# Seven products in place of eight also for the second matrix product of the experts

## The chip, the cores and the metric

The kernel runs on one core of a Trainium2 chip. The metric is device time of one execution in microseconds; the median of three runs of the kernel before is 2268.2 us (2265.57 to 2270.24). The profile comes from one further execution, which took 2266.92 us.

## The reference

Three layers follow each other on 2304 tokens of 512 features: attention with a memory (4 batches, 8 heads, 576 positions), a gated feed-forward layer, and a dense mixture of 8 experts. The change is in the mixture:

```
logits = x @ w_gate;  P = exp(logits - max), then 8 times rows and columns normalised (Sinkhorn)
for e in range(8):
    h = maximum(x @ w1[e], 0)          # 2304x512 @ 512x1024
    out += P[:, e:e+1] * (h @ w2[e])   # 2304x1024 @ 1024x512
```

All is float32. Each matrix product is computed as three products of rounded parts: a number is split into a high part (rounded to the fast matmul's format) and a low part (the rest), and high x high, high x low and low x high are added.

## The kernel before, in words

The mixture (moe2) works through 16 units: a unit is half of an expert's 1024 hidden features, 512 of them. In a unit it goes through four pairs of 512 tokens and a last group of 256 tokens.

**Hidden products.** x W1 of a pair is a product of 2x2 blocks by the Strassen-Winograd scheme, with seven products in place of eight (unit_hidden). Operands are blocks (A11, A12, A21, A22) of W1 and sums of them (S1 to S4), and seven parts of x per pair. The seven parts of x are made once, written to DRAM by parts (L583), and read back for each unit into five right-side buffers (xr, L1027). One such product is 12 matmuls with 256 moving columns and a new 128x128 stationary tile each (L904). Results gather in PSUM: a bank named chain (pool pc), and banks of pool pt. ScalarE copies the chain aside (keep, L911), VectorE adds (L916), ScalarE takes relu into the high part of h (L923), and VectorE makes its low part (L924). For the last 256 tokens (last_hidden, L956) all eight block products are made, 48 matmuls.

**Output products.** h W2 is computed without the scheme (unit_out, L976): 128 tokens by 512 output features, 12 matmuls with 512 moving columns, in one bank of pool poc, called an output chunk below. VectorE adds the bank, scaled by the token's weight, to the accumulator of the outputs (L992, in unit 0 a copy, L988).

**Order.** moe2 writes the order of TensorE's queue out by hand: "HHOHHOHHOHO" for a pair, H a hidden product of this pair and O an output chunk of the pair before; "HOOHOO" for the last 256 tokens. After each letter a step of other work may be issued (behind): the next unit's weights (prepare_unit, L819) or, in unit 0, the logits, the fourth pair's parts of x, and the Sinkhorn steps. prepare_unit loads 2 MB of raw weights through SP's queue (L825), GpSimd makes S1 to S4 (L845), ScalarE the high parts (L834, L839), VectorE and GpSimd the low parts (L835, L841). Engines run their own queues in order; tc.issue_after fixes a place in the queue only, it isn't a wait.

## Time and profile before

| | us |
|---|---|
| median of three runs | 2268.2 |
| profiled execution | 2266.92 |
| its span in the profile | 2264.8 |
| first hidden product of the mixture starts at | 723.13 |
| second unit starts at | 836.87 |

The span is the part of the execution that the profile covers, and times inside it count from its start. Busy times of engines overlap; a matmul's duration in the timeline includes its way through the array, so consecutive matmuls overlap, and the spacing of their starts is what they cost. A row of the timeline merges equal neighbours ("x12"), its idle time before them and what ended it stand in brackets.

### The profile page before, as it was taken

The numbers are of one execution on the slowest core, as the hardware profiler recorded it, in microseconds if no ns is written. First come the engines' busy times: TensorE is split into PE (matmuls) and PEld (weight loads), VectorE is DVE, ScalarE is ACT, GpSimd is POOL, SyncE is SP. The second block draws the span as 40 slices with busy tenths as digits, with TensorE's granted clock in tenths as the row PEclk, the third lists the DMA queues.
The fourth block names the chain that finished last, engine by engine and source line by source line (L and its number), as shares of the span: only waits on it lengthen the run. The fifth ranks groups of instructions, "written<-read, shape, count | busy, mean of one in ns | idle before, by whom it ended". The sixth has DMA issues, their size and how long they took to land.

```text
span 2264.8 us, 33872 instructions
## 1 busy us (share of the span) xinstructions
PE 2219.6 (98%) x13490; PEld 1904.9 (84%) x13490; DVE 1205.4 (53%) x1915; ACT 735.0 (32%) x1452; POOL 466.7 (21%) x425
## 2 busy tenths in 40 slices
PE   7999999999999899999999999999999999999999
PEld 4555677888888789989899898998989989899898
DVE  8999898442413655444454444544445444454433
ACT  6777733322312312222222222222222222232221
POOL 6766665210201121101011010110101101011000
PEclk9999999999999999999999999999999999999999
DMA  5322276357533836546465464654646546465463
GB/s 188 119 93 78 100 253 214 132 203 259 199 118 117 282 112 233 197 148 224 148 230 197 150 223 146 229 195 156 223 144 230 196 157 218 146 229 199 159 203 132
DMA packets 112956, 406.46 MB, mean 179 GB/s; under 512 B 12448, under 2 KB 12448, under 8 KB 109728
## 3 DMA queue, kind: packets, MB, share of 16 engines
q1 hardware_dynamic: 112800, 404.30, 52.5%
q8 instruction: 108, 1.77, 0.3%
q14 instruction: 48, 0.39, 0.1%
HBM read 364.92 MB, written 39.32 MB: 178 GB/s over the span
## 4 chain that ended last, share of the span: by engine, by line
PE 80%; DVE 2%; DMA 2%; POOL 1%; issue 1%; ACT 0%; SPq 0%; POOLq 0%; ACTq 0%; DVEq 0%
PE po L474 39%; PE pt L904 15%; PE pc L904 11%; PE p L474 9%; PE pt L967 4%; DMA xp<-xl 1%; DMA raw<-w 1%; POOL na L503 1%; PE pp L474 1%; POOL ws L845 0%; DVE na L488 0%; DVE w L835 0%; DMA graw<-gvo 0%; DVE nb L491 0%; DVE nb L492 0%
## 5 line engine op out<-in xcount | busy, mean ns | idle before, releaser
L474 PE MATMUL po<-w,h 128*128 128x512 f32 x3456 | 834.4, 392 | 4.2 <-DVE xacc L988 4.2
L474 PEld LDWEIGHTS po<-w,h 128*128 128x128 f32 x3456 | 631.8, 188 | 126.2 <-DVE xacc L988 4.5
L904 PE MATMUL pt<-xr,w 128*128 128x256 f32 x3072 | 403.8, 280 | 5.0 <-DMA xr<-xp 4.9
L904 PEld LDWEIGHTS pt<-xr,w 128*128 128x128 f32 x3072 | 381.7, 188 | 13.6 <-DVE w L841 5.1
L992 DVE SCALAR_TENSOR_TENSOR xacc<-po,Pw,xacc 128x512 f32<-128x512 f32 x270 | 202.2, 749 | 272.2 <-PE po L474 272.1
L474 PE MATMUL p<-xs,gw 128*128 128x512 f32 (+1 forms) x1440 | 306.9, 370 | 6.5 <-DVE sg L639 3.6
L904 PEld LDWEIGHTS pc<-xr,w 128*128 128x128 f32 x2304 | 296.8, 188 | 15.0 <-ACT m L911 0.2
L904 PE MATMUL pc<-xr,w 128*128 128x256 f32 x2304 | 304.3, 280 | 0.0
L474 PEld LDWEIGHTS p<-xs,gw 128*128 128x128 f32 x1440 | 251.9, 189 | 55.3 <-DVE sg L639 4.9
L911 ACT COPY m<-pc 128x512 f32<-128x512 f32 x192 | 112.2, 584 | 510.0 <-PE pc L904 509.8
L916 DVE TENSOR_TENSOR m<-pt,m 128x512 f32<-128x512 f32 x256 | 175.0, 688 | 182.8 <-PE pt L904 121.3
L923 ACT ACTIVATE h<-m 128x512 fp32r<-128x512 f32 x256 | 161.4, 633 | 263.5 <-DVE m L916 256.3
L924 DVE SCALAR_TENSOR_TENSOR h<-m,h 128x512 fp32r<-128x512 f32 x256 | 191.8, 754 | 70.5 <-ACT h L923 65.8
L835 POOL TENSOR_TENSOR w<-raw,w 128x512 fp32r<-128x512 f32 x17 | 22.5, 1323 | 755.0 <-ACT w L834 755.0
L841 POOL TENSOR_TENSOR w<-raw,w 128x512 fp32r<-128x512 f32 x32 | 57.3, 1792 | 472.1 <-ACT w L839 472.1
L474 PE MATMUL po<-h,ws 128*128 128x512 f32 x576 | 137.4, 390 | 0.0
L474 PEld LDWEIGHTS po<-h,ws 128*128 128x128 f32 x576 | 108.0, 188 | 23.0
L835 DVE TENSOR_TENSOR w<-ws,w 128x512 fp32r<-128x512 f32 x64 | 66.4, 1039 | 79.3 <-ACT w L834 77.0
L322 POOL TENSOR_SCALAR P<-P,sums 128x576 f32<-128x576 f32 (+4 forms) x160 | 92.3, 591 | 26.4 <-ACT Z L392 12.1
L503 POOL TENSOR_SCALAR na<-na 128x512 f32<-128x512 f32 x36 | 87.1, 2434 | 47.6 <-ACT na L502 47.4
L967 PEld LDWEIGHTS pt<-xr,w 128*128 128x128 f32 x768 | 94.4, 188 | 2.7
L967 PE MATMUL pt<-xr,w 128*128 128x256 f32 x768 | 95.3, 279 | 0.0
(186 smaller groups left out, 1930.2 us busy)
## 6 DMA issues: line engine op xcount, KB each, us to landing
xr<-xp SPq DMA_DIRECT2D x480, 512.0 KB, 4.1
raw<-w SPq DMA_DIRECT2D x64, 512.0 KB, 6.1
gw<-kg SPq DMA_DIRECT2D x24, 1024.0 KB, 4.8
graw<-gvo SPq DMA_DIRECT2D x36, 512.0 KB, 4.3
xp<-xl SPq DMA_DIRECT2D x30, 512.0 KB, 3.3
kg<-gw SPq DMA_DIRECT2D x24, 512.0 KB, 3.9
ws<-ko SPq DMA_DIRECT2D x24, 512.0 KB, 3.8
qk<-qkv SPq DMA_DIRECT2D x16, 640.0 KB, 3.9
```

The costliest lines, as they stand in the source:

```text
L322: nc.gpsimd.tensor_scalar(t, t, r, 1.0, op0=ALU.mult, op1=ALU.mult)
L474: self.nc.tensor.matmul(out, lhs[a], rhs[b], start=start and n == 0, stop=stop and n == 2, skip_group_check=shared)
L503: nc.gpsimd.tensor_scalar(t, t, pattern(0x40000000), pattern(0x4FEFFE00), op0=ALU.max, op1=ALU.min)
L835: lo.tensor_sub(t[:, 1], q[name], f32(t[:, 0]))
L841: engine.tensor_sub(t[:, 1, j], raw[:, 2 * n + j, 1], f32(t[:, 0, j]))
L904: nc.tensor.matmul(out[:, j * HT:(j + 1) * HT], w[:, a, j, k], x[:, b, k], start=start and j + k + n == 0, stop=k + n == 3, skip_group_che ...
L911: nc.scalar.copy(t, src)
L916: nc.vector.tensor_add(c, *terms)
L923: nc.scalar.activation(t[:, 0], c, AF.Relu)
L924: nc.vector.scalar_tensor_tensor(t[:, 1], c, 0.0, f32(t[:, 0]), op0=ALU.max, op1=ALU.subtract)
L967: nc.tensor.matmul(ph[:, j * HT:(j + 1) * HT], w[:, b, j, k], x[:, c, k], start=j + a + k + i == 0, stop=a + k + i == 4, skip_group_check= ...
L992: nc.vector.scalar_tensor_tensor(acc, po, weight, acc, op0=ALU.mult, op1=ALU.add)
```

## The change

h W2 of units 1 to 15 is now a product of 2x2 blocks with seven products as well. The blocks of h (A11, A12, A22; A21 only within sums) and the sums s1 to s4 of them are the stationary side; blocks of W2 (B11, B21, B22) and sums T1 to T4 are the moving side, 256 columns wide. unit_out is a generator: each step issues one product for a pair (two times 128 tokens, 12 matmuls) or for the last 256 tokens (6 matmuls), and two or one accumulations of 128x256 from PSUM into the outputs. The banks pu and pq hold partial results that go on being added to after they have been read. Unit 0 keeps whole chunks (first_out).

The hidden products come in the order A11, A12, S2, S1, S4, S3, A22; S2, S1 and S4 add to the chain, A22 adds to the bank of S3. A letter H begins with tick, which issues low parts and sums put off from the letters before (later). The order is "HO" seven times, "HOOHOOHOOHO" for the last 256 tokens; unit 0 keeps its own for pairs. prepare_unit has gates: after S3, S2, T3 and B11 it waits for the last 256 tokens (1), and before T2, T4, T1, B21, B22 for the next unit's first pair (2). PSUM is split into four pools of two banks (pu, pq, pt, pc). In unit 0 the fourth pair's parts come before the logits. The core of the diff:

```diff
--- before.py
+++ after.py
@@ -602,13 +602,13 @@
         yield
         t3 = new()
         sub(t3, b22, b12)
-        self.part(pool, t4, to[5])
-        yield
-        self.part(pool, t3, to[4])
+        self.part(pool, t4, to[6])
+        yield
+        self.part(pool, t3, to[5])
         yield
         self.part(pool, b21, to[1])
         yield
-        self.part(pool, b22, to[6])
+        self.part(pool, b22, to[4])
         yield
     def moe1(self, last):
...
     def prepare_unit(self, u):
+        low = []
+        for gate in self.unit_steps(u, low):
+            yield gate
+            while low:
+                low.pop(0)()
+        for what in low:
+            what()
+    def unit_steps(self, u, low):
...
+        q = {}
+        for i in range(2):
+            for j in range(2):
+                q[f"A{i + 1}{j + 1}"] = raw[:, 2 * i:2 * i + 2, 0, j * HT:(j + 1) * HT]
+                q[f"B{i + 1}{j + 1}"] = raw[:, 2 * i:2 * i + 2, 1, j * HT:(j + 1) * HT]
+        def split(t, src, lo):
+            nc.scalar.copy(t[:, 0], src)
+            low.append(lambda: lo.tensor_sub(t[:, 1], src, f32(t[:, 0])))
+        def parts(name, lo=nc.vector):
+            w1[name] = self.w1p.tile([P, 2, 2, HT], F32R, name="w1")
+            split(w1[name], q[name], lo)
+        def parts2(name, lo=nc.vector):
+            t = self.w2p.tile([P, 2, 512], F32R, name="xl")
+            w2[name] = t.rearrange("p a (j n) -> p a j n", j=2)
+            split(w2[name], q[name], lo)
...
+        for _ in range(8 if u else 0):
             yield
+        total("S3", sub, "A11", "A21")
+        yield
+        parts("S3")
+        yield
+        total("S1", add, "A21", "A22")
+        yield
+        total("S2", sub, "S1", "A11")
+        yield
+        parts("S2")
+        yield
+        total("S4", sub, "A12", "S2")
+        yield
...
+        total("T3", sub, "B22", "B12")
+        parts2("B11", nc.gpsimd)
+        yield
+        parts2("T3")
+        yield
+        yield 1
+        for name in ("A11", "A12", "S1", "S4", "A22"):
+            parts(name)
             yield
+        total("T1", sub, "B12", "B11")
         parts("A21", nc.gpsimd)
         yield
+        total("T2", sub, "T1", "B22")
+        yield
+        yield 2
+        parts2("T2")
+        total("T4", add, "B21", "T2")
+        yield
+        parts2("T4")
+        yield
+        parts2("T1")
+        yield
+        parts2("B21", nc.gpsimd)
+        yield
+        parts2("B22")
+        yield
+    def later(self, steps, what):
+        self.todo.append((self.now + steps, what))
+    def tick(self):
+        self.now += 1
+        due = [t for t in self.todo if t[0] <= self.now]
+        self.todo = [t for t in self.todo if t[0] > self.now]
+        for _, what in due:
+            what()
+    def split_h(self, h, name, src, relu, n=512):
+        t = self.hp.tile([P, 2, 512], F32R, name="h")[:, :, 0:n]
+        if relu:
+            nc.scalar.activation(hi, src, AF.Relu)
+            self.later(1, lambda: nc.vector.scalar_tensor_tensor(lo, src, 0.0, f32(hi), op0=ALU.max, op1=ALU.subtract))
+        else:
+            nc.scalar.copy(hi, src)
+            self.later(1, lambda: nc.vector.tensor_sub(lo, src, f32(hi)))
...
         chain = self.pc.tile([P, 512], F32, name="pc")
         one = lambda: self.pt.tile([P, 512], F32, name="pt")
         mm(chain, "A11", xs(0), True)
         m1 = keep(chain)
-        yield h
+        yield
         m2 = one()
         mm(m2, "A12", xs(1), True)
-        result((0, 0), m2, m1)
-        yield h
+        c11 = plus(m2, m1)
+        self.split_h(h, "A11", c11, True)
+        yield
         mm(chain, "S2", xs(2))
         u2 = keep(chain)
-        split()
-        mm(chain, "S3", xs(4))
+        yield
+        mm(chain, "S1", xs(3))
         u3 = keep(chain)
...
+        mm(chain, "S4", xs(4))
+        if u:
+            r21 = new()
+            nc.scalar.activation(r21, chain, AF.Relu)
+        yield
+        m7 = one()
+        mm(m7, "S3", xs(5), True)
+        if u:
+            s3 = new()
+            relu(s3, c11, r21, ALU.subtract)
+            self.split_h(h, "S3", s3, False)
+        c22 = plus(m7, u3)
+        self.split_h(h, "A22", c22, True)
+        yield
+        mm(m7, "A22", xs(6))
+        if u:
+            s1 = r21
+            relu(s1, c22, r21, ALU.add)
+            self.split_h(h, "S1", s1, False)
+        c21 = plus(m7, u2)
+        self.split_h(h, "A12", c21, True)
+        def rest():
+            s2 = c11
+            relu(s2, c11, s1, ALU.subtract)
+            self.split_h(h, "S2", s2, False)
+            def last():
+                s4 = c21
+                relu(s4, c21, s2, ALU.add)
+                self.split_h(h, "S4", s4, False)
+            self.later(1, last)
+        if u:
+            self.later(1, rest)
+        yield
...
+                if j == 0:
+                    yield
+            t = self.mp.tile([P, 512], F32, name="m")
+            nc.scalar.activation(t, ph, AF.Relu)
+            r.append(t.rearrange("p (j t n) -> p j t n", j=2, t=2))
+            if i == 0:
+                (a11, a21) = (r[0][:, :, k] for k in range(2))
+                self.split_h(h, "A11", a11, False, n)
+                s3 = self.half_tile()
+                nc.vector.tensor_sub(s3, a11, a21)
+                self.split_h(h, "S3", s3, False, n)
+            else:
+                (a12, a22) = (r[1][:, :, k] for k in range(2))
+                s1 = self.half_tile()
...
+    def first_out(self, p, h, t, c):
...
+    def unit_out(self, u, p, h):
...
+        for a, b, bank, i, d in (
+            ("A11", "B11", "pu", 0, 0), ("S3", "T3", "pq", 1, 1), ("S2", "T2", "pu", 1, 0), ("A22", "T4", "pq", 1, 0),
+            ("S1", "T1", "pu", 1, 1), ("A12", "B21", "pq", 0, 0), ("S4", "B22", "pu", 0, 1),
+        ):
+            start = bank not in banks or a == "A12"
+            if start:
+                banks[bank] = getattr(self, bank).tile([P, 2, HT], F32, name=bank)[:, 0:m]
+            po = banks[bank]
+            for c in range(m):
+                for j in range(2):
+                    for n, (x, y) in enumerate(((0, 0), (0, 1), (1, 0))):
+                        nc.tensor.matmul(
+                            po[:, c], h[a][:, x, j, c * P:(c + 1) * P], w2[b][:, y, j],
+                            start=start and c + j + n == 0, stop=j + n == 3, skip_group_check=True,
+                        )
+            for c, at in enumerate(rows[i]):
+                acc = self.acc[:, at, d * HT:(d + 1) * HT]
+                self.marks[2] = nc.vector.scalar_tensor_tensor(
+                    acc, po[:, c], self.Pw[:, at, e:e + 1], acc, op0=ALU.mult, op1=ALU.add
+                )
...
+            xrp, self.hp, w2p, self.mp, sk = (
+                pool(n, b, side="right") for n, b in (("xr", 4), ("hc", 8), ("w2", 7), ("m", 9), ("sk", 1))
             )
-            self.po, self.pt, self.pc = (pool(n, b, space=PSUM) for n, b in (("poc", 3), ("pt", 3), ("pc", 2)))
             xl = self.xl
+            self.w2p = Pools((w2p, 7), (xl, 2))
+            self.pu, self.pq, self.pt, self.pc = (pool(n, 2, space=PSUM) for n in ("pu", "pq", "pt", "pc"))
...
                 yield from self.parts(PAIRS2 - 1)
                 t0 = 2 * HT * PAIRS2
                 for n in range(2):
                     self.part(xl, self.x[:, 2 * n:2 * n + 2, t0:NT], self.xparts[PAIRS2][n])
                     yield
-                yield from self.sinkhorn(sk, self.po)
+                for c in range(2, len(CHUNKS1)):
+                    yield from self.logits(self.pu, "pu", xl, *(sum(CHUNKS1[c][0:k]) // P for k in (1, 2)))
+                yield from self.sinkhorn(sk, self.pu)
...
-                    while len(tiles) < min(n + 5, len(stream)):
+                    while len(tiles) < min(n + 4, len(stream)):
...
+                with ExitStack() as order:
+                    for mark in filter(None, self.marks):
+                        order.enter_context(tc.issue_after(mark.ins))
                     return next(steps, None)
+            self.marks = [None] * 3
...
-                        hidden, order = self.unit_hidden(u, p, right(u, p)), "HHOHHOHHOHO"
+                        hidden, order = self.unit_hidden(u, h, right(u, p)), "HO" * 7 if u else "HHOHHOHHOHO"
                     else:
-                        hidden, order = self.last_hidden(u, right(u, p)), "HOOHOO"
+                        hidden, order = self.last_hidden(u, h, right(u, p)), "HOOHOOHOOHO" if u else "HOHOHOHO"
+                    free = 1 if p == PAIRS2 else 2 if p == 0 and u else 0
                     for at, what in enumerate(order):
                         if what == "H":
-                            h = next(hidden)
+                            self.tick()
+                            next(hidden)
+                        if p == 1 and at == (6 if u == 0 else 0):
                             for _ in prep:
                                 pass
-                            prep = self.prepare_unit(u + 1) if u + 1 < UNITS else iter(())
+                            prep, gate = self.prepare_unit(u + 1) if u + 1 < UNITS else iter(()), 0
+                        if gate <= free and (what == "O" or free < 2) and (u or p):
+                            gate = behind(prep) or gate
...
             while pend:
-                self.unit_out(*pend.pop(0))
+                self.tick()
+                pend.pop(0)()
```

## Rows read from the trace of the kernel before

**Rows 1.** The page, part 1: busy us, share of the span, instructions.

```profile
PE 2219.6 (98%) x13490; PEld 1904.9 (84%) x13490; DVE 1205.4 (53%) x1915; ACT 735.0 (32%) x1452; POOL 466.7 (21%) x425
```

**Rows 2.** Windows view, one mid-run unit; engine busy (instructions), clock, DMA share, GB/s.

```profile
1498.70:1593.20 94.50, 94.50 (x601) 85.44 (x600) 44.38 (x61) 24.88 (x40) 10.41 (x7) 1.00 0.57 190
```

**Rows 3.** Timeline of that unit, TensorE: start us, us, engine, line, operation, count.

```profile
1498.70 1.56 PE L904 MATMUL pc<-xr,w 128*128 128x256 f32 x12
1500.10 1.56 PE L904 MATMUL pt<-xr,w 128*128 128x256 f32 x12
1501.49 2.92 PE L474 MATMUL po<-w,h 128*128 128x512 f32 x12
1504.25 1.56 PE L904 MATMUL pc<-xr,w 128*128 128x256 f32 x12
...
1576.68 2.96 PE L967 MATMUL pt<-xr,w 128*128 128x256 f32 x24
1579.47 5.64 PE L474 MATMUL po<-w,h 128*128 128x512 f32 x24
1584.95 2.96 PE L967 MATMUL pt<-xr,w 128*128 128x256 f32 x24
...
1593.22 1.56 PE L904 MATMUL pc<-xr,w 128*128 128x256 f32 x12
```

**Rows 4.** Instruction groups by form after 700 us: busy us, mean ns, idle before.

```profile
L474 PEld LDWEIGHTS po<-w,h 128*128 128x128 f32 x3456 | 631.8, 188 | 126.2 <-DVE xacc L988 4.5
...
L992 DVE SCALAR_TENSOR_TENSOR xacc<-po,Pw,xacc 128x512 f32<-128x512 f32 x270 | 202.2, 749 | 272.2 <-PE po L474 272.1
...
L916 DVE TENSOR_TENSOR m<-pt,m 128x512 f32<-128x512 f32 x256 | 175.0, 688 | 182.8 <-PE pt L904 121.3 <-ACT m L911 60.1
...
L911 ACT COPY m<-pc 128x512 f32<-128x512 f32 x192 | 112.2, 584 | 510.0 <-PE pc L904 509.8
...
L845 POOL TENSOR_TENSOR ws<-raw 128x512 f32<-128x512 f32 x30 | 38.7, 1291 | 25.6 <-DMA raw<-w 17.5 <-DVE xacc L988 6.8 <-DVE xacc L992 1.3
L834 ACT CAST w<-raw 128x512 fp32r<-128x512 f32 x60 | 37.3, 621 | 90.7 <-PE pt L967 50.0 <-PE pt L904 40.7
...
L835 DVE TENSOR_TENSOR w<-raw,w 128x512 fp32r<-128x512 f32 x45 | 30.9, 687 | 2.3 <-ACT w L834 2.3
...
L558 DVE TENSOR_TENSOR xl<-xacc,xl 128x256 fp32r<-128x256 f32 x4 | 1.7, 418 | 0.0
```

**Rows 5.** Timeline, VectorE with instructions waiting in its queue.

```profile
1527.83 0.74 DVE L992 SCALAR_TENSOR_TENSOR xacc<-po,Pw,xacc 128x512 f32<-128x512 f32 x1
1528.49 0.68 DVE L835 TENSOR_TENSOR w<-ws,w 128x512 fp32r<-128x512 f32 x1
1529.09 1.28 DVE L916 TENSOR_TENSOR m<-pt,m 128x512 f32<-128x512 f32 x2
```

**Rows 6.** Timeline, VectorE and GpSimd side by side.

```profile
1509.76 1.80 POOL L841 TENSOR_TENSOR w<-raw,w 128x512 fp32r<-128x512 f32 x1 [23.32 <-ACT w L839]
...
1510.32 0.74 DVE L992 SCALAR_TENSOR_TENSOR xacc<-po,Pw,xacc 128x512 f32<-128x512 f32 x1
...
1518.97 1.79 POOL L841 TENSOR_TENSOR w<-raw,w 128x512 fp32r<-128x512 f32 x1 [7.41 <-ACT w L839]
1519.53 1.78 DVE L924 SCALAR_TENSOR_TENSOR h<-m,h 128x512 fp32r<-128x512 f32 x1
```

**Rows 7.** Timeline, a product and the instruction that its predecessor releases.

```profile
1505.65 1.56 PE L904 MATMUL pt<-xr,w 128*128 128x256 f32 x12
1505.91 0.59 ACT L911 COPY m<-pc 128x512 f32<-128x512 f32 x1 [2.79 <-PE pc L904]
...
1517.02 2.94 PE L474 MATMUL po<-w,h 128*128 128x512 f32 x12
1517.28 0.69 DVE L916 TENSOR_TENSOR m<-pt,m 128x512 f32<-128x512 f32 x1 [0.34 <-PE pt L904]
```

**Rows 8.** The page, part 6: DMA issues, KB each, us to landing.

```profile
xr<-xp SPq DMA_DIRECT2D x480, 512.0 KB, 4.1
raw<-w SPq DMA_DIRECT2D x64, 512.0 KB, 6.1
```

**Rows 9.** Windows view, four us with the raw weights landing.

```profile
1520.00:1524.00 4.00, 4.00 (x31) 3.74 (x30) 1.97 (x2) 0.59 (x1) 2.93 (x3) 1.00 1.03 418
```

**Rows 10.** Timeline, first unit; the last row begins the second unit.

```profile
723.13 1.56 PE L904 MATMUL pc<-xr,w 128*128 128x256 f32 x12
...
755.31 0.62 ACT L579 CAST xl<-ws 128x512 fp32r<-128x512 f32 x1 [1.72 <-DMA xp<-xl]
...
767.85 2.90 PE L904 MATMUL pt<-xr,w 128*128 128x256 f32 x12 [4.89 <-DMA xr<-xp]
774.98 7.15 PE L474 MATMUL po<-w,h 128*128 128x512 f32 x24 [4.23 <-DVE xacc L988]
...
836.87 1.10 PE L904 MATMUL pc<-xr,w 128*128 128x256 f32 x8
```

**Rows 11.** Chain of waits at the end: start us, us, what.

```profile
2250.05 10.92 PE po L474 x48
2260.96 0.02 issue
2260.99 0.75 DVE xacc L992
```

More of the change, by code (lines that the diff above doesn't have):

```diff
@@ L730, in moe1 @@
                     po = new(n)
-                    self.rawp, self.w1p = (pool(k, b, last) for k, b in (("raw", 1), ("w1", 11)))
+                    self.rawp, self.w1p = (pool(k, b, last) for k, b in (("raw", 1), ("w1", 10)))
                 weights(1, f)
@@ L744, in moe1 @@
             self.prep0 = self.prepare_unit(0)
-            aside += [more(2, False), iter(lambda: next(self.prep0), "late")]
+            aside += [more(2, False), iter(lambda: next(self.prep0), 2)]
             banks.close()
@@ L857, in prepare_unit @@
         yield
-        parts("S2", nc.vector)
-        yield
-        total("S3", sub, "A11", "A21")
-        parts("S3", nc.vector)
+        parts("S2")
         yield
@@ L864, in prepare_unit @@
         yield
-        parts("S1", nc.vector)
-        yield
-        if first:
-            parts("A22", nc.gpsimd)
-            yield
-            parts("S4", nc.vector)
-            yield
-            parts("A21", nc.gpsimd)
-            yield "late"
-            parts2(0)
-            parts2(1)
-            return
-        parts2(0)
-        yield
-        yield "late"
-        parts("S4", nc.vector)
-        yield
-        for name in ("A11", "A12", "A22"):
-            parts(name, nc.vector)
-            yield
+        if u == 0:
+            for name in ("A11", "A12", "S1", "S4", "A22", "A21"):
+                parts(name, nc.gpsimd if name[1] == "2" else nc.vector)
+                yield
+            yield 2
+            for n in range(4):
+                w2[n] = self.w2p.tile([P, 2, 512], F32R, name="xl")
+                split(w2[n], raw[:, n, 1], nc.vector)
+            return
@@ L897, in mm, with unit_hidden @@
+    def unit_hidden(self, u, h, xs):
+        nc, w1 = self.nc, self.w1[u]
+        new = lambda: self.mp.tile([P, 512], F32, name="m")
         def mm(out, name, xt, start=False):
@@ L985, in unit_out @@
[L985 to L994 removed]
+                hs = h[f"A{t + 1}{n + 1}"][:, :, j, c * P:(c + 1) * P]
@@ L1061, in moe2 @@
-                        if p == PAIRS2 and at or p < PAIRS2 and (p, at) > (u == 0, 6) and not late:
-                            late = behind(prep) == "late" or late
-                    for _ in hidden:
-                        pass
+                            prep, gate = self.prepare_unit(u + 1) if u + 1 < UNITS else iter(()), 0
+                        if gate <= free and (what == "O" or free < 2) and (u or p):
+                            gate = behind(prep) or gate
                     if u == p == 0:
```

158 lines of the change are left out of this document (73 added, 85 removed).

## The prediction

> **What bounds the kernel now.** First the busy times: TensorE is busy for 98% of the span, VectorE for 53%, ScalarE for 32%, GpSimd for 21% [rows 1]. Only TensorE can be the bound, but a share is a mean over stages, so next one unit is cut out with the windows view. In a mid-run unit TensorE is busy 94.50 of 94.50 us at full granted clock, VectorE 44.38 (61 instructions), ScalarE 24.88, GpSimd 10.41 [rows 2]. Then the timeline of that unit: each hidden product (x W1, 12 matmuls of 256 columns) starts 1.40 us after the one before it, each output chunk (h W2, 12 matmuls of 512 columns) takes 2.75, 24 of them 5.47, and the unit repeats after 1593.22 - 1498.70 = 94.52 us [rows 3]. There is no gap to see: 32 x 1.40 + 18 x 2.75 = 94.3. So in 15 of the 16 units a column not streamed is time saved, until another engine is late.
>
> **What the change removes.** Only units 1 to 15 get the seven-product h W2; unit 0 keeps whole chunks. A pair of 512 tokens has now 4 chunks, 48 matmuls of 512 columns, 11.0 us; after it 7 products of 12 matmuls of 256 columns. Matmuls of 256 columns whose stationary tile is new each time are what the hidden products are: 1.40 / 12 = 117 ns, against 2.75 / 12 = 229 ns for 512 [rows 3]. The fixed part of a matmul is thus some 4 ns, and halving it costs nearly nothing. A product is 1.40 us, a pair 9.8. Per unit (four pairs and the last 256 tokens, whose products are 0.70): 31.5 x 1.40 = 44.1 instead of 18 x 2.75 = 49.5. Saved: 5.4 us a unit, 81 us in 15 units. The hidden products are reordered, not fewer.
>
> The Trainium skill ("TensorE: Matmul & The Clock Gate", Back-to-back issue gap) speaks against this: in streams of weight load and matmul it gives about 81 ns a matmul at 128 columns and 131 at 512, because the load counts too. An estimate between these two, 98 ns at 256, would make the new form cost 378 x 98 = 37 us a unit against 216 x 131 = 28, and the kernel some 130 us slower. The trace disagrees on both sizes (117 and 229), and the measurement decides.
>
> **What it adds, on VectorE.** A pair had 12 wide instructions there (4 sums, 4 low parts, 4 accumulations). It gets 3 sums, 4 combinations of relu results, 7 low parts, and 14 accumulations of half width. Alone a wide one takes 0.69 us (accumulation 0.75) [rows 4], but in a queue they start 0.60 apart, an accumulation 0.66 [rows 5]. The half-width accumulation is not in the trace. Half-width VectorE instructions take 0.42 where wide ones take 0.69 [rows 4], so it is 0.75 - 0.27 = 0.48 alone and 0.66 - 0.27 = 0.39 in a queue; ends 0.33 and 0.75, and I take 0.39, since VectorE will have a queue. A pair is 14 x 0.60 + 14 x 0.39 = 13.9 us, below its 19.6 of TensorE. The last tokens add 11 half-width instructions at 0.33 and 7 accumulations, 6.4; the weights 12 low parts, 7.2. Unit: 55.6 + 6.4 + 7.2 = 69 us (at full durations 82), against 44 now. GpSimd gets 11 wide instructions of 1.29 instead of 7 [rows 4], 14 us. ScalarE gets 59 wide copies a unit at 0.62, and nine small ones: about 40 us, no bound.
>
> GpSimd and VectorE stand in each other's way: a VectorE instruction with both inputs in SBUF took 1.78 us beside a GpSimd one, ending 0.55 after it, while an accumulation, with one input in PSUM, took its usual 0.74 beside another [rows 6]. So each of 11 GpSimd instructions can cost VectorE from 0 to 1.29 us. Most of them (four weight sums) run when the raw weights have landed, about the fourth slot of the second pair, where VectorE has only accumulations; I charge 6 us. VectorE: 75 of 90 us. Hence TensorE stays the bound, with hand-offs that show where VectorE or ScalarE is late.
>
> **The new waits.** A slot is one hidden and one output product, 2.80 us (2.10 in the first pair of a unit, where the output product is that of 256 tokens). An engine starts 0.26 us after the product that releases it [rows 7]; then 0.59 for a ScalarE copy, 0.69 for a sum [rows 4]. Three hidden products now add to a bank that the neighbour before has just filled, after a copy or sum has read it: S1 after S2, S4 after S1, A22 after S3. Between them stands one output product, 1.40 us, which covers 0.26 + 0.59 and 0.26 + 0.69. VectorE's order in a full pair, from the end of the product before: two accumulations to 1.0, three wide (two low parts and s2) to 2.8; the first output product ends at 2.80, its accumulations at 3.85; low part of S2, s4 and the sum for A11 to 5.65. That sum's relu copy holds ScalarE to 6.4; S2 ends at 7.0, its bank's copy at 7.85, and S1 is due at 8.4. So 0.5 us is left, and the second and fourth pairs have no stall. Elsewhere:
> - First pair: cover 0.70. The same order puts the sum for A11 to 5.1 and its copy to 5.8, a weight copy (T4) stands next to 6.4, then the bank's copy to 7.0; S1 is due at 6.3 and starts some 0.8 late. S4 0.2; A22 0.26 + 0.69 - 0.70, so 0.3. Together 1.3 us.
> - Third pair: a weight low part and one GpSimd instruction (0.60 + 1.29) come before the sum for A11, of which 0.5 is covered and 0.9 falls into VectorE's idle time: S1 about 0.5 late.
> - Last tokens: the low parts of two weights stand ahead of the low part of S2, and its output product, with two output products and one hidden one as cover, starts about 0.9 late (low part done at 6.45, product due at 5.6).
>
> Sum 2.7 us a unit; ends 0 (all covered) and 7 (96.0 a unit, below). A unit takes 94.5 - 5.4 + 2.7 = 91.8.
>
> **Queues and buffers.** Bytes stay; right-side buffers fall from 5 to 4. SP issues the four raw loads in the first slots of the second pair between the right-side loads; these still lead by 4 x 2.8 - 1.4 = 9.8 us, 7.0 in the first pair, and land in 4.1, raw loads in 6.1 [rows 8]. A burst of 418 GB/s cost TensorE nothing [rows 9]. If VectorE is late with the last raw reader, the raw load holds SP, and 5.7 us of that are covered. Nothing charged.
>
> **Once only.** Unit 0 takes 836.87 - 723.13 = 113.7 us now, with two stops, 4.89 for a right-side load and 4.23 for VectorE, while the parts of the fourth pair are still being stored [rows 10]. Storing them before the logits takes these 9 us away. But ScalarE waits for stores before further copies (1.72 in that row [rows 10]), and these copies now stand in the first pair, where S1, S4 and A22 need ScalarE and VectorE and no output product covers: I put its 9.8 us of products at 20. Then S1 follows S2 directly in each later pair, 0.26 + 0.59 each. Net +3 us (from -9, only the stops, to +15, the stops staying and 6 more). The logits and the balancing of the token weights come later; they have 52 steps of unit 0 for their 41, so unit 1's accumulations don't wait. In unit 1's first pair only two output products exist: three bare hand-offs, 2.4 us. At the end now 10.92 us of output chunks run after the last hidden product and 0.75 of accumulation [rows 11]; after it s2, s4 and their copies and low parts, some 0.4 each in half width, are on the path: +2 (0 to 4).
>
> **Sum.** Profiled execution 2266.9 (span 2264.8): 15 x 2.7 = 40.5 less, 7.4 more: 2233.8. The median of the runs is 1.3 above that execution: 2235.
>
> **Rivals.**
> *No hand-off shows.* For it: three of four hand-offs have a cover longer than their duration. Against it: the 0.70 of the first pair. 15 x 5.4 = 81 less and about 5 more: 2192.
> *The gain is used up.* Hand-offs of 5 us a unit, by twice as many late copies in the first pair and last tokens; for it, ScalarE and VectorE serve in strict order and one late copy holds the next. 15 x 0.4 = 6 less and 7 more: 2269.
> *VectorE becomes the bound (slower).* Place: first pair, third pair and last tokens, where low parts meet GpSimd. If queued instructions cost their full durations, 82 us, and each GpSimd instruction blocks its whole 1.29, 14 us, a unit needs 96.0 us of VectorE; it decides from 94.5 on. 15 x 1.5 + 7 = +30: 2298. For it: the 1.78 [rows 6]. Against it: the 0.60 spacing [rows 5], and that 17 of a pair's 28 instructions read PSUM. The Trainium skill ("SBUF — State Buffer", SBUF: two separate sides) has the same lock, exclusive and held for the whole instruction, also against VectorE instructions with two SBUF inputs; the 1.78 agrees.
> *The load sets the pace.* If matmuls on freshly written stationary tiles were spaced by the 188 ns of a load [rows 4], 378 x 0.188 = 71 us a unit instead of 49.5: 2590. Against it: 117 in the hidden products. This is how the skill's rule above would act.
>
> **How the numbers follow.** Forecast 0.58, its own range 2212 to 2262 (1.2 to 4.5 us of hand-offs); no hand-off 0.17; gain used up 0.09; VectorE the bound 0.15; load 0.01. A measurement tells 0.2%, 4.5 us, from no change. Faster: 0.58 + 0.17 + 0.03 = 0.78; same 0.05; slower 0.17. The range, 2190 to 2272, holds the first three.
>
> **What would show it.** Output products of 12 matmuls starting 1.40 after each other, VectorE at 70 to 80 us a unit, a unit of about 92 us, with idle TensorE before S1, S4 and A22 in the first pair, and before S2's output product in the last tokens. Wrong if a unit's VectorE has no idle time, or if output products are over 1.5 us apart with nothing waited for.

## The result and the profile after

The changed kernel takes 2227.26 us (median of four runs, 2223.35 to 2228.96), the kernel before 2268.17 beside it. The ratio is 0.9818 with the interval 0.9801 to 0.9835: 41 us faster, 8 us below the forecast of 2235 and inside its own range. The profiled execution after took 2223.35 us, its span 2221.6, so the span is 43.2 us shorter where the sum had 33.1. One run of x_unit0b below took 7334.14 us and is left out of its median and range.

The page, part 1, of the changed kernel, beside [rows 1]:

```profile
PE 2169.4 (98%) x15920; PEld 1978.7 (89%) x15920; DVE 1651.7 (74%) x3128; ACT 943.9 (42%) x1874; POOL 561.1 (25%) x483
```

TensorE is still busy 98% of the time. VectorE rose from 53% to 74%, ScalarE from 32% to 42%, GpSimd from 21% to 25%. The windows view of one unit after, columns as in [rows 2]:

```profile
1514.30:1605.80 91.50, 91.06 (x763) 90.35 (x763) 73.39 (x143) 38.79 (x69) 16.42 (x11) 1.00 0.57 196
```

The window is one period of 91.5 us. VectorE has 73.4 us of it (forecast 75, with 142 instructions), ScalarE 38.8 (about 40), GpSimd 16.4 (14). VectorE has 18 us to spare over the unit; it isn't the bound.

The timeline of TensorE in the steady part of a pair after, beside [rows 3]:

```profile
1425.72 1.59 PE L954 MATMUL pc<-xr,w 128*128 128x256 f32 x12
1427.14 1.59 PE L1119 MATMUL pu<-xl,h 128*128 128x256 f32 x12
1428.57 1.57 PE L954 MATMUL pt<-xr,w 128*128 128x256 f32 x12
1429.98 1.60 PE L1119 MATMUL pq<-xl,h 128*128 128x256 f32 x12
1431.41 1.57 PE L954 MATMUL pc<-xr,w 128*128 128x256 f32 x12
```

Hidden (L954) and output products (L1119) alternate without a wait, a slot (one hidden and one output product) takes 2.84 us, where 2.80 was forecast. The starts of single matmuls, averaged over units 2 to 14, are 119.2 ns apart in the output products and 117.2 in the hidden ones; an output matmul of 512 columns before stood 229.1 from the next.

Where the 43 us come from, by the start of the first hidden product of each unit in the two profiled executions:

| stretch | before | after | difference | forecast |
|---|---|---|---|---|
| up to the first hidden product | 723.13 | 726.46 | +3.3 | 0 |
| unit 0 | 113.74 | 116.43 | +2.7 | +3 |
| unit 1 | 94.10 | 93.11 | -1.0 | -0.3 |
| units 2 to 14, each | 94.60 | 91.10 | 13 x -3.50 = -45.5 | 13 x -2.7 = -35.1 |
| unit 15 and the end | 103.95 | 101.23 | -2.7 | -0.7 |

The column sums to -43.2. Most of the difference to the forecast is in the repeated unit; ahead of the units there is a loss that the prediction had not seen.

**The first pair of a unit.** The timeline of all engines after, with TensorE's first two stops:

```profile
1484.90 0.69 DVE L966 TENSOR_TENSOR m<-pt,m 128x512 f32<-128x512 f32 x1
...
1485.67 0.63 ACT L847 CAST xl<-ws 128x512 fp32r<-128x512 f32 x1 [1.19 <-PE pq L1119]
...
1486.20 0.63 ACT L935 ACTIVATE h<-m 128x512 fp32r<-128x512 f32 x1
...
1486.82 0.87 PE L1119 MATMUL pu<-xl,h 128*128 128x256 f32 x6
...
1487.02 0.59 ACT L961 COPY m<-pc 128x512 f32<-128x512 f32 x1 [0.20 <-PE pc L954]
...
1487.66 1.67 PE L954 MATMUL pc<-xr,w 128*128 128x256 f32 x12
...
1489.17 0.87 PE L1119 MATMUL pq<-xl,h 128*128 128x256 f32 x6
...
1490.00 1.69 PE L954 MATMUL pc<-xr,w 128*128 128x256 f32 x12
...
1491.53 0.88 PE L1119 MATMUL pu<-xl,h 128*128 128x256 f32 x6
```

A product of six matmuls takes some 0.71 us. S1 (1487.66) starts 0.84 after it began, S4 (1490.00) 0.83: 0.13 and 0.12 late. The two are then slower themselves: the next product follows after 1.51 and 1.53 us instead of 1.41, since their second matmul starts some 0.22 us after the first instead of 0.12. So each of the two costs 0.23 us in all, where 0.8 and 0.2 were forecast. What a stop costs is given below in this way: what the starts of the matmuls around it exceed their usual spacing by, averaged over units 2 to 14.

The sum for A11 (L966) runs 0.20 us after its product and ends 4.4 us after the start of the pair's first product (1481.16), where 5.1 was forecast. T4's weight copy (L847, 1485.67) and A11's relu copy (L935) are done at 1486.83, and the copy of the bank (L961) then waits for nothing but S2 itself; it starts 0.20 after the product behind S2 has begun.

A22 is stopped as well, for 0.24 us, with VectorE's sum in the same view:

```profile
1493.64 0.88 PE L1119 MATMUL pq<-xl,h 128*128 128x256 f32 x6
1493.74 0.69 DVE L939 TENSOR_TENSOR h<-m,h 128x512 fp32r<-128x512 f32 x1 [0.29 <-ACT h L938]
1494.35 0.68 DVE L966 TENSOR_TENSOR m<-pt,m 128x512 f32<-128x512 f32 x1
1494.36 0.76 PE L1119 MATMUL pu<-xl,h 128*128 128x256 f32 x5
...
1495.09 1.66 PE L954 MATMUL pt<-xr,w 128*128 128x256 f32 x12
```

Two output products, not one, run between S3 and A22 here, the second but for its last matmul. The sum that frees the bank (L966) starts 0.71 us after the first of them, not some 0.2, because the low part of s3 (L939) stands in front of it.

**The second pair.** A stop that the prediction denied:

```profile
1510.07 1.30 POOL L861 TENSOR_TENSOR ws<-ws,raw 128x512 f32<-128x512 f32 x1
1510.34 1.57 DVE L970 SCALAR_TENSOR_TENSOR m<-m 128x512 f32<-128x512 f32 x1 [1.22 <-ACT m L992]
...
1511.45 1.63 POOL L861 TENSOR_TENSOR ws<-raw,ws 128x512 f32<-128x512 f32 x1
...
1512.63 1.00 DVE L939 TENSOR_TENSOR h<-m,h 128x512 fp32r<-128x512 f32 x1
1513.55 0.68 DVE L966 TENSOR_TENSOR m<-pt,m 128x512 f32<-128x512 f32 x1
...
1514.28 1.68 PE L954 MATMUL pt<-xr,w 128*128 128x256 f32 x12 [0.39 <-DVE m L966]
```

Read it from the bottom. A22's product waits 0.39 us for VectorE's sum (L966), which frees the bank. That sum stands in VectorE's queue behind s3 (L970) and its low part (L939); s3 took 1.57 us and the low part 1.00 instead of 0.68, both with two inputs in SBUF, both beside a sum of the next unit's weights on GpSimd (L861). This stop isn't in every unit: it costs 0 to 0.87 us, 0.32 on average.

**Ahead of the units**, in the gated layer, after:

```profile
577.62 1.26 POOL L861 TENSOR_TENSOR ws<-raw 128x512 f32<-128x512 f32 x1
578.92 0.62 ACT L847 CAST w<-ws 128x512 fp32r<-128x512 f32 x1 [5.27 <-POOL ws L861]
579.44 0.59 ACT L638 ACTIVATE sg<-p 128x512 f32<-128x512 f32 x1
...
580.09 5.88 PE L474 MATMUL p<-xs,gw 128*128 128x256 f32 x36 [2.40 <-ACT sg L638]
```

ScalarE stands 5.27 us at a weight copy of unit 0, since GpSimd hasn't made that sum (S3) yet. Behind it in the queue is the activation (L638) that TensorE needs, and TensorE stands 2.40 us. Before, the same activation started at 575.02.

### The profile page after: what moved, and what is told of

Same layout as the page of the kernel before. It is cut to its first block, busy times and chain, and to the rows that moved or that the text cites. A ratio compares the mean times of both kernels' runs of the same rounds, so it can differ in the third digit from the quotient of the medians.

```text
span 2221.6 us, 40559 instructions
## 1 busy us (share of the span) xinstructions
PE 2169.4 (98%) x15920; PEld 1978.7 (89%) x15920; DVE 1651.7 (74%) x3128; ACT 943.9 (42%) x1874; POOL 561.1 (25%) x483
## 4 chain that ended last, share of the span: by engine, by line
PE 76%; DVE 4%; DMA 3%; POOL 1%; issue 1%; ACT 1%; SPq 0%; POOLq 0%; DVEq 0%; ACTq 0%
PE pu L1119 16%; PE pc L954 15%; PE pq L1119 12%; PE pt L954 11%; PE p L474 9%; PE po L474 5%; PE pt L1042 4%; PE pq L474 2%; DMA raw<-w 2%; PE pp L474 1%; DMA xr<-xp 1%; POOL ws L861 0%; POOL na L503 0%; DVE na L488 0%; DVE m L966 0%
## 5 line engine op out<-in xcount | busy, mean ns | idle before, releaser
L1119 PE MATMUL pu<-xl,h 128*128 128x256 f32 x3240 | 437.3, 282 | 1.1 <-DVE xacc L1125 1.1
L954 PE MATMUL pc<-xr,w 128*128 128x256 f32 x3072 | 408.9, 282 | 4.0 <-DMA xr<-xp 3.9
L1119 PEld LDWEIGHTS pu<-xl,h 128*128 128x128 f32 x3240 | 408.3, 190 | 1.4 <-issue 1.4
L954 PEld LDWEIGHTS pc<-xr,w 128*128 128x128 f32 x3072 | 381.3, 189 | 12.2 <-ACT m L961 6.0
L1119 PE MATMUL pq<-xl,h 128*128 128x256 f32 x2430 | 326.4, 282 | 0.0
L954 PE MATMUL pt<-xr,w 128*128 128x256 f32 x2304 | 305.0, 281 | 3.9 <-DVE m L966 2.4
L1119 PEld LDWEIGHTS pq<-xl,h 128*128 128x128 f32 x2430 | 305.8, 190 | 0.0
L954 PEld LDWEIGHTS pt<-xr,w 128*128 128x128 f32 x2304 | 284.4, 188 | 9.2 <-DVE m L966 6.6
L938 ACT CAST h<-m 128x512 fp32r<-128x512 f32 (+1 forms) x345 | 189.0, 556 | 217.6 <-DVE m L970 208.0
L1125 DVE SCALAR_TENSOR_TENSOR xacc<-pu,Pw,xacc 128x256 f32<-128x256 f32 x540 | 237.4, 476 | 40.2 <-PE pu L1119 38.2
L1125 DVE SCALAR_TENSOR_TENSOR xacc<-pq,Pw,xacc 128x256 f32<-128x256 f32 x405 | 178.5, 477 | 110.6 <-PE pq L1119 109.8
L970 DVE SCALAR_TENSOR_TENSOR m<-m 128x512 f32<-128x512 f32 x240 | 174.5, 727 | 77.5 <-ACT m L992 76.0
L939 DVE TENSOR_TENSOR h<-m,h 128x512 fp32r<-128x512 f32 (+1 forms) x345 | 208.6, 615 | 10.0 <-ACT h L938 8.6
L935 ACT ACTIVATE h<-m 128x512 fp32r<-128x512 f32 x192 | 121.5, 633 | 175.6 <-DVE m L966 174.0
L861 POOL TENSOR_TENSOR ws<-raw 128x512 f32<-128x512 f32 x62 | 88.6, 1440 | 409.5 <-DMA raw<-w 171.4
L961 ACT COPY m<-pc 128x512 f32<-128x512 f32 x192 | 112.5, 586 | 185.3 <-PE pc L954 185.3
L966 DVE TENSOR_TENSOR m<-pt,m 128x512 f32<-128x512 f32 x192 | 131.4, 684 | 4.2 <-PE pt L954 4.0
```

The costliest lines, as they stand in the source:

```text
L935: nc.scalar.activation(hi, src, AF.Relu)
L938: nc.scalar.copy(hi, src)
L939: self.later(1, lambda: nc.vector.tensor_sub(lo, src, f32(hi)))
L954: nc.tensor.matmul(out[:, j * HT:(j + 1) * HT], w[:, a, j, k], x[:, b, k], start=start and j + k + n == 0, stop=k + n == 3, skip_group_che ...
L961: self.marks[1] = nc.scalar.copy(t, src)
L966: nc.vector.tensor_add(t, a, b)
```

## The experiments

A unit is below the mean period of units 2 to 14, with lowest and highest; the kernels are named as in the headings. What lies ahead of the mixture varies by some us from run to run (the first hidden product starts at 726.46 and 728.02 in the two profiles of the changed kernel), so unit periods tell small effects better than totals.

**Again.** The changed kernel with nothing edited.

> The changed kernel again, as the yardstick for the three others on this chip. All theories: 2227 us, ratio to the kernel before 0.980 to 0.984.

2227.44 us (2224.29 to 2229.13), ratio 0.9809 (0.9795 to 0.9822); a unit 91.24.

**Whole output chunks (x_whole).** h W2 goes back to 12 matmuls of 512 columns; the new order of the hidden products, the four pools and the order in unit 0 stay.

```diff
-        hidden, order = self.unit_hidden(u, h, right(u, p)), "HO" * 7 if u else "HHOHHOHHOHO"
+        hidden, order = self.unit_hidden(u, h, right(u, p)), "HHHOHOHHOHO" if u else "HHOHHOHHOHO"
...
-                w = self.w2[0][2 * n + j]
+                w = self.w2[u][2 * n + j]
...
+            self.marks[2] = nc.vector.scalar_tensor_tensor(acc, po, weight, acc, op0=ALU.mult, op1=ALU.add)
```

> Undoes one part: h W2 goes back to whole chunks of 512 columns in all units (no sums of h, no sums of W2), while the new order of the hidden products, the four pools of two banks, the deferred low parts and the four right-side buffers stay. Order of a pair HHHOHOHHOHO, so that a chunk covers each hand-off. Theory (the gain is the columns saved): 32 x 1.41 + 18 x 2.75 = 94.6, and 0.9 in the first pair where no chunk stands between S3 and A22: 95.5 a unit, 4.4 above the changed kernel's 91.1; 2280 to 2295. Rival (the gain comes from the order, the banks or the queues): 2225 to 2250.

2283.77 us (2280.67 to 2284.52), ratio 1.0055 (1.004 to 1.007); a unit 95.04 (94.57 to 95.9). TensorE's timeline:

```profile
1400.91 2.96 PE L474 MATMUL pq<-xl,h 128*128 128x512 f32 x12
1403.70 1.56 PE L1027 MATMUL pt<-xr,w 128*128 128x256 f32 x12
```

The wide product is back, at 2.79 us. Without the seven products everything else of the change is a loss of 0.5%; with them a unit is 3.9 us shorter. So the gain goes with the seven products and not with the order, the banks or the queues. (The edit also takes away the work that the seven products add on the other engines.)

**Twice the low parts (x_low4, x_low7, x_low7_nosums).** Four, then all seven, of h's low parts are made twice on VectorE: how far is it from being the bound? In the third kernel, GpSimd's sums of weights of units 1 to 15 are left out as well (raw blocks take their place).

```diff
-            self.later(1, lambda: nc.vector.tensor_sub(lo, src, f32(hi)))
+        def low():
+            for _ in range(2 if name in ("A11", "S3", "S2", "A12") else 1):
+                ...
+        self.later(1, low)
```

> Doubles a suspected cost: VectorE computes four of the seven low parts of h (A11, S3, S2, A12) twice, 10.9 us more of VectorE a unit (4 x 4 x 0.60 + 4 x 0.33), 74 to 85 of 91. Theory (TensorE is the bound, VectorE only makes hand-offs late): 0.5 to 2 us more a unit, 2235 to 2257. Rival (VectorE already sets the end): 10.9 x 15 = 164 more, 2390. Second rival (VectorE has slack everywhere): 2227.

2251.6 us (2250.01 to 2254.02), ratio 0.9917 (0.99 to 0.9934); a unit 93.12: 10.9 us more work on VectorE (16 wide instructions by 0.60, four of half width by 0.33) cost 2.0 us a unit.

> As before with all seven low parts twice: 19 us more of VectorE a unit, 74 to 93, above the 91.1 of a unit. Theory: VectorE is now the bound, 93 to 97 a unit, 2255 to 2315, no idle time on VectorE. Rival (VectorE already sets the end): 2510. Second rival (slack): 2227 to 2235.

2349.49 us (2345.41 to 2354.05), ratio 1.0348 (1.0328 to 1.0368); a unit 99.24 (97.63 to 102.48). Missed: VectorE is the bound, as expected, but 34 us beyond the range. The next kernel was to tell whether GpSimd holds it up.

> All seven low parts of h twice, and GpSimd's eight weight sums of units 1 to 15 left out (raw blocks in their place, so the outputs differ). With the sums this took 98.5 us a unit and 2349, beyond the 93 that VectorE's queue spacing gave. Theory (with VectorE the bound, what GpSimd blocks is paid in full: 8 sums of up to 0.7 us each): 94 to 95 a unit, 2285 to 2300. Rival (it is hand-offs between VectorE, ScalarE and TensorE that a late VectorE adds, whatever GpSimd does): 97.5 to 98.5, 2335 to 2350.

2283.83 us (2281.44 to 2284.72), ratio 1.0061 (1.0047 to 1.0074); a unit 95.10. The windows view from 1300 to 1700 us, x_low7 and then x_low7_nosums, columns as above:

```profile
1300.00:1700.00 400.00, 376.95 (x3064) 367.34 (x3065) 388.26 (x714) 151.28 (x273) 68.28 (x45) 1.00 0.54 181
```

```profile
1300.00:1700.00 400.00, 387.17 (x3206) 380.95 (x3205) 388.71 (x746) 155.94 (x283) 16.79 (x13) 1.00 0.55 184
```

In both VectorE is busy 97% of the time; TensorE's busy time is 94% and 97%, but it waits for VectorE in both (from 950 to 2110 us for low parts of h alone 20.5 us in x_low7 and 22.8 in x_low7_nosums). Without the sums VectorE gets through 746 instructions in the same 388 us instead of 714. The instruction groups by form from 950 to 2110 us (mean ns is the number behind the comma), x_low7:

```profile
L944 DVE TENSOR_TENSOR h<-m,h 128x512 fp32r<-128x512 f32 x374 | 271.5, 726 | 0.0
L942 DVE SCALAR_TENSOR_TENSOR h<-m,h 128x512 fp32r<-128x512 f32 x282 | 213.9, 759 | 0.0
...
L977 DVE SCALAR_TENSOR_TENSOR m<-m 128x512 f32<-128x512 f32 x188 | 142.8, 760 | 16.0 <-ACT m L999 16.0
...
L973 DVE TENSOR_TENSOR m<-pt,m 128x512 f32<-128x512 f32 x142 | 96.6, 680 | 2.1 <-PE pt L961 2.1
```

and x_low7_nosums:

```profile
L948 DVE TENSOR_TENSOR h<-m,h 128x512 fp32r<-128x512 f32 x392 | 266.9, 681 | 0.0
L946 DVE SCALAR_TENSOR_TENSOR h<-m,h 128x512 fp32r<-128x512 f32 x294 | 200.6, 682 | 0.0
...
L981 DVE SCALAR_TENSOR_TENSOR m<-m 128x512 f32<-128x512 f32 x196 | 134.0, 684 | 20.6 <-ACT m L1003 20.5
L977 DVE TENSOR_TENSOR m<-pt,m 128x512 f32<-128x512 f32 x147 | 100.4, 683 | 0.0
```

The two low parts and the combinations of relu results (both inputs in SBUF) go from 726, 759 and 760 ns to 681, 682 and 684 on average, the sum that reads PSUM stays at 680 to 683. Over the 11.7 units in this stretch that is (374 x 45 + 282 x 77 + 188 x 76) / 11.7 = 4.5 us of VectorE a unit. The eight sums cost 99.24 - 95.10 = 4.1 us a unit here, some 0.5 each, which fits VectorE paying for them in full. Not all of the overrun is theirs: without them a unit is still 4.0 us over the changed kernel's. A part goes with late loads of the right side, 1.4 and 0.9 us a unit, as TensorE's waits in the same stretch show, x_low7 and then x_low7_nosums (us in total, times, longest):

```profile
PE pt L961 <- DMA xr<-xp: 16.0, 20, 1.1
```

```profile
PE pt L965 <- DMA xr<-xp: 11.2, 13, 1.1
```

**No sums, nothing else (x_nosums).**

```diff
+            if u:
+                q[name] = q[a]
+            else:
+                op(q[name], q[a], q[b])
```

> GpSimd's eight weight sums of units 1 to 15 are left out (a raw block stands in for each sum, so the outputs differ). Theory (GpSimd holds VectorE back only where its sums meet s3 and the sum for A22, some 0.35 us a unit on average): 2219 to 2224. Rival (the two block each other at large, 6 us a unit as the prediction charged, and TensorE feels it): 2140 to 2190.

2216.75 us (2216.23 to 2218.12), ratio 0.9764 (0.9749 to 0.9778). A unit is 90.79, and all 13 lie between 90.73 and 90.87: the unevenness of the changed kernel (90.73 to 91.71) goes with the sums. In none of these 13 units is there a stop in the second pair, while those in the first pair are as before. In the profiles unit 0, whose second half prepares unit 1, is 2.1 us shorter, unit 1 0.8, units 2 to 14 together 4.0. While TensorE is the bound, the sums cost 0.3 to 0.45 us a unit.

**The first pair's order (x_first_pair).** One more hidden product ahead, so that two output products of 256 tokens stand between S2 and S1, S1 and S4, S3 and A22.

```diff
-                        hidden, order = self.unit_hidden(u, h, right(u, p)), "HO" * 7 if u else "HHOHHOHHOHO"
+                        hidden, order = self.unit_hidden(u, h, right(u, p)), ("HO" * 7 if p else "HHHOOHOOHOHOOH") if u else "HHOHHOHHOHO"
```

> Only the order of products in a unit's first pair is changed (HHHOOHOOHOHOOH in place of HO seven times), so that two half-size output products (1.42 us together) stand where one (0.71) stood between S2 and S1, S1 and S4, S3 and A22. Theory (the cover of 0.7 is too short for a copy or a sum, 0.2 + 0.59 or 0.69): the spacing of S1 and S4 after it falls by 0.13 and 0.12, that of A22 by 0.2 to 0.3, a unit by 0.5, 15 units by 7 us: 2220. Rival (VectorE's and ScalarE's queues are late there whatever stands between): units keep 91.1 us, 2227; second rival (output products bunched, so accumulations come late and stall the banks): 2230 to 2240.

2222.05 us (2221.79 to 2222.6), ratio 0.9787 (0.9774 to 0.98), but a unit 91.04 against 91.10 and 91.24 in the two profiles of the changed kernel. That is 0.1 to 0.2 a unit, less than expected, and the interval overlaps that of x_after. The stops at S1 and S4 are gone, 0.46 us a unit. But the one at A22 has grown:

```profile
1495.54 0.69 DVE L939 TENSOR_TENSOR h<-m,h 128x512 fp32r<-128x512 f32 x1 [0.29 <-ACT h L938]
1495.83 0.87 PE L1119 MATMUL pu<-xl,h 128*128 128x256 f32 x6
1496.15 0.68 DVE L966 TENSOR_TENSOR m<-pt,m 128x512 f32<-128x512 f32 x1
...
1496.89 1.67 PE L954 MATMUL pt<-xr,w 128*128 128x256 f32 x12 [0.18 <-DVE m L966]
```

VectorE's sum (L966), which frees the bank, again stands behind the low part of s3 (L939), and A22 starts 1.06 us after the output product before it instead of 0.71. This stop costs 0.45 us a unit where it cost 0.24, and the one in the second pair 0.51 (0.32 and 0.46 in the two profiles of the changed kernel). So the edit moved most of the stopped time to the next place where VectorE's queue is late.

**Unit 0's weights (x_unit0, x_unit0b).** First try: A11 and A12 are prepared first, then S3 as in the changed kernel.

```diff
+        if u == 0:
...
+            for name in ("A11", "A12"):
+                parts(name)
+                yield
```

> Only unit 0's weight preparation is changed: high parts of A11 and A12, which need no GpSimd, come first again, then S3 and the rest. Theory (the 3.1 us that the changed kernel lost before the first hidden product come from ScalarE waiting 5.27 us for GpSimd's S3 ahead of the gated layer's activation): the first hidden product starts at 723 in place of 726.5, and the time is 2224. Rival (the loss comes from more copies in that place, whatever their order): 726 and 2227.

2227.49 us (2224.41 to 2230.0), ratio 0.9815 (0.9801 to 0.9828). From 550 us to the first hidden product it takes 176.16, as before the edit (176.14), and ScalarE stands 5.27 us at the same copy of S3. The edit didn't move that copy away from the activation: missed. Second try: the order of the kernel before, in which S1 and S2 are summed first, and no copy needs S1 yet.

```diff
+            total("S1", add, "A21", "A22")
+            yield
+            total("S2", sub, "S1", "A11")
+            yield
+            parts("S2")
+            yield
+            total("S3", sub, "A11", "A21")
+            parts("S3")
```

> Unit 0's weight preparation in exactly the order of the kernel before (A11, A12, then S1, S2, its copy, then S3). The first try moved A11 and A12 alone, and the 5.27 us of ScalarE behind GpSimd's S3 stayed. Theory (the copy of S3, issued one step after a sum that GpSimd can start only after four other sums, stands in ScalarE's queue ahead of the activation): from the row at 550 us to the first hidden product 172.7 us as before in place of 176.0, and the time 2224. Rival (something else in that stretch): 176 and 2227.

2222.37 us (2220.93 to 2223.14), ratio 0.9789 (0.9776 to 0.9802). The same place in its timeline:

```profile
575.88 0.60 ACT L638 ACTIVATE sg<-p 128x512 f32<-128x512 f32 x1 [1.42 <-PE p L474]
...
582.08 0.62 ACT L847 CAST w<-ws 128x512 fp32r<-128x512 f32 x1 [1.61 <-POOL ws L862]
```

The activation again comes ahead of the copy that waits for a sum, and the stretch takes 172.82 us, as in the kernel before (172.84). So the 3.3 us come from the order in which unit 0's weights are prepared; that it is the one waiting copy is read from the two timelines, since the edit puts the whole order back.

**The matmul's spacing (x_spacing).** In the first pair's output products the stationary tile is replaced by one of W1's, in the second pair's the moving one.

```diff
+                        if p == 0:
+                            still = self.w1[u]["A22"][:, x, j, c * P:(c + 1) * P]
+                        elif p == 1:
+                            moving = self.w1[u]["A22"][:, y, j]
```

> Measures the disputed spacing by itself: matmuls of output products start 120 ns apart, those of hidden products 116.5, with 256 columns both. For the first pair of each unit the stationary side of the output products is a W1 tile in place of h, for the second pair the moving side is a W1 tile in place of W2's (outputs differ), the third and fourth stay. If the stationary tile makes it, the first pair's fall to 116.5 and the second's stay at 120; if the moving tile, the other way round; if it is neither (the banks, the queue), both stay at 120. No theory ahead; the prediction took 116.5 for all.

One run, 2220.97 us. The mean distance of matmuls within output products is 117.6 ns with the stationary tile swapped, 118.2 with the moving one swapped, 119.2 in the pairs left alone; in hidden products 117.0 to 117.4, the stopped ones left out. Of the 2 ns between the two kinds, the stationary tile brings 1.6 back and the moving one 1.0. None of the outcomes named ahead came true: both tiles count. Banks and places in the queue are the same in all four pairs, so they alone don't make the difference. What it is about the tiles, their place or what they hold, stays open.

**All mends together (x_all, x_best).** x_all: the first pair's order, the first try on unit 0, and in the second stop's place the low part of s3 put behind the sum that frees the bank:

```diff
-            self.later(1, lambda: nc.vector.tensor_sub(lo, src, f32(hi)))
+            def low():
+                with ExitStack() as order:
+                    if after:
+                        order.enter_context(self.tc.issue_after(after[0].ins))
+                    nc.vector.tensor_sub(lo, src, f32(hi))
...
+            self.split_h(h, "S3", s3, False, after=sum22)
```

> Both edits together and a third: the low part of s3 is put behind the sum for A22 in VectorE's queue. Theory: 3.2 from unit 0, 7 from the first pairs, and 0.35 a unit, 4.5, where GpSimd's weight sums delay that sum (units of 91.5 in place of 90.8): 2212. Rival (the long units come from something other than that low part): 2217. If VectorE is the real bound: no better than 2224.

2217.34 us (2214.73 to 2220.98), ratio 0.9767 (0.9752 to 0.9782); a unit 90.51: with the sum moved ahead a unit is 0.5 shorter than in x_first_pair. In the first pair no stop is left, also none at A22, and those in the second and third pairs cost 0.19 together. The total is the rival's 2217 all the same: the first try on unit 0 brought nothing and the first pair's order alone little. x_best takes the second try on unit 0 instead.

> All that helped, with unit 0's preparation in the order of the kernel before: the first pair's order, the low part of s3 behind the sum for A22. Theory: 3.2 below the kernel that had the first try for unit 0 (2217): 2214. Rival: 2217.

2213.08 us (2211.7 to 2214.03), ratio 0.975 (0.9737 to 0.9763); a unit 90.65. It beats both kernels, the changed one by 14 us. Its first pair in TensorE's timeline:

```profile
1486.97 1.57 PE L978 MATMUL pt<-xr,w 128*128 128x256 f32 x12
1488.38 0.88 PE L1147 MATMUL pq<-xl,h 128*128 128x256 f32 x6
1489.10 0.87 PE L1147 MATMUL pu<-xl,h 128*128 128x256 f32 x6
1489.81 1.57 PE L978 MATMUL pt<-xr,w 128*128 128x256 f32 x12
```

Every start follows at the spacing of the products themselves, 1.41 and 0.71 to 0.72; no stop is left in it. What is left in a unit are 0.33 us in the second and third pairs and a new stop of 0.24 in the last tokens.

## Why the prediction was right, and where its sizes were off

The forecast case came true: TensorE stays the bound, columns not streamed are time saved, VectorE fills up without taking over. A unit was forecast at 91.8 us and is 91.1. Behind that agreement are two errors that partly cancel: the columns save 1.2 us a unit less than forecast, and the hand-offs cost 2.0 less.

- **The columns, saved 5.4 a unit in the forecast, 4.2 measured** (91.10 less 1.03 of stops after, 94.60 less 0.29 before). The step "the fixed part of a matmul is thus some 4 ns, and halving it costs nearly nothing" was mis-sized. It compared the hidden stream (117 ns at 256 columns) with the output stream (229 at 512). Within the output stream the halved matmul takes 119.2, so 2 x 119.2 - 229.1 = 9 ns are fixed. A slot is 2.84 instead of 2.80; with 31.5 of them a unit that is 1.3 us. x_whole against the changed kernel gives 3.9. In both streams the starts are 117 to 119 ns apart at full granted clock, so the rival that the load sets the pace, at 188 ns, is out. The Trainium skill ("TensorE: Matmul & The Clock Gate", Back-to-back issue gap) led to an estimate of 98 ns at 256 columns; the trace doesn't bear it out.
- **The hand-offs, 2.7 a unit in the forecast, 0.7 measured** (1.03 less 0.29). In the first pair S1 and S4 cost 0.23 each and A22 0.24, 0.7 together where 1.3 was forecast. The 0.8 at S1 failed at "the same order puts the sum for A11 to 5.1 and its copy to 5.8, a weight copy (T4) stands next to 6.4": VectorE's queue isn't late there, the sum ends at 4.4, the weight copy stands in front of the relu copy, and both are done when S2 ends. What remains is the bare hand-off, 0.20 + 0.59, against a cover of 0.71. The third pair and the last tokens have no stop; the forecast low parts and weights don't stand ahead of what TensorE waits for. That the forecast of A22 (0.3) agrees is luck: it took a bare hand-off against one output product; in the trace nearly two cover it, and the sum is late behind the low part of s3. With that low part put behind the sum (x_all, against x_first_pair) the stop is gone.
- **GpSimd and VectorE.** "About the fourth slot of the second pair, where VectorE has only accumulations" failed: s3 and its low part are there, and A22's sum behind them. The price is small, 0.3 to 0.45 a unit by x_nosums, about the size of the stop in the second pair (0.32 and 0.46), which is gone without the sums. The 6 us charged to VectorE aren't there either. In x_nosums, from 1300 to 1700 us:

```profile
1300.00:1700.00 400.00, 400.00 (x3355) 397.36 (x3355) 320.93 (x625) 172.33 (x302) 19.41 (x13) 1.00 0.60 204
```

  That is 72.8 us of VectorE in a unit of 90.79; the changed kernel has 322.93 us in the same stretch, 73.5 in a unit of 91.10. So the sums cost VectorE 0.7 us a unit.
- **VectorE as the bound.** 73.4 to 74.7 us of 91.5 were measured against 75. That this agrees is in part luck: without what GpSimd costs it, VectorE is busy 72.8 us and not 69. A half-width accumulation takes 476 ns on the profile's page (0.48 forecast), two in a queue 0.87 (0.39 apart, as taken). The rival needed 96 us; x_low4 (VectorE 370 of 400 us busy) and x_low7 show that it is real and where it starts: 10.9 us more cost 2.0 a unit, 19.1 (28 and 7 instructions) cost 8.1. There the blocking is dear: 4.1 us a unit come from the sums. The means of 726 and 759 ns in the low parts, beside 680 in the sum that reads PSUM, show which instructions are held up. The Trainium skill ("SBUF — State Buffer", SBUF: two separate sides) says that the lock concerns VectorE instructions with two SBUF inputs; these means agree.
- **Once only.** Unit 0 +2.7 (+3 forecast), in part by luck. The first pair takes 15.3 us up to the end of its last hidden product (726.46 to 741.75) and not 20. But of the two stops that were to go, only the one for VectorE went; TensorE still waits 4.6 us for right-side loads (4.89 before):

```profile
749.15 1.64 PE L954 MATMUL pt<-xr,w 128*128 128x256 f32 x12 [1.37 <-DMA xr<-xp]
754.04 1.66 PE L954 MATMUL pc<-xr,w 128*128 128x256 f32 x12 [3.25 <-DMA xr<-xp]
```

  Unit 1 is 2.0 over a normal unit (2.4). The last stretch gains 0.8 less than a normal unit (2.0); its last stops for VectorE are 0.41 and 0.67 us:

```profile
2213.39 0.47 PE L1119 MATMUL pu<-xl,h 128*128 128x256 f32 x2 [0.41 <-DVE xacc L1125]
...
2217.05 0.95 PE L1119 MATMUL pu<-xl,h 128*128 128x256 f32 x6 [0.67 <-DVE xacc L1125]
```

- **Missed: 3.3 us ahead of unit 0.** The prediction followed the moved weight steps only through the mixture. unit_steps also feeds unit 0, in the gated layer, and there its first step is now a sum with a copy behind it. With the old order in x_unit0b the 3.3 us are gone.

In sum, units 2 to 14 give 13 x 0.80 = 10.4 us more than forecast, units 1 and 15 some 2.7, unit 0 0.3, and the missed stop takes 3.3: -43 where -33 stood.

## What to carry to other kernels

Take a matmul's fixed cost from two sizes in one stream, not from two streams: some 2.5 ns an output matmul (378 of them, 0.9 us a unit) are most of the 1.2 us that were missing from the expected 5.4. When a helper that prepares data is reordered, follow each of its callers: a loss of 3.3 us lay in another layer, where a copy that waits for a slow engine stood in front of an activation. In a strict queue, what frees a bank for the bounding engine belongs ahead of work that only must be done some time (x_all, 0.5 us a unit). And count the stops of a whole unit after an edit, not only those that it aims at: x_first_pair took 0.46 us away and put most of it back further on.

## What was not expected of the hardware

The distance of matmuls with 256 columns depends, by up to 2 ns of 117, on the tiles that they read (x_spacing); the cause stays open. A product that TensorE starts late loses some 0.1 us more between its first and second matmul. And the same eight GpSimd sums cost 0.3 to 0.45 us a unit while TensorE is the bound, 4.1 once VectorE is.
